# A fixed TensorE order for the experts' products, and one DVE place a unit for the weights' block sums

## Chip, cores and metric

One core of one Trainium2 chip. The metric is the device time of one execution in microseconds (us). The kernel before took 996.0 us in the median of three runs (993.51 to 996.29), and 994.75 us in the median of four.

## The reference, cut to what matters

```python
def _attn_ref(q, k, v):                     # linear attention, 8 batches x 8 heads x 576 x 64
    ...
def _moe_ref(x, w_gate, w1, w2):            # x: attention's output, 4608 x 512; 8 experts, hidden width 1024
    ...
    P = np.exp(logits)                      # logits from x @ w_gate; then 8 rounds of row and column scaling
    ...
    for e in range(E):
        h = np.maximum(x @ w1[e], 0.0)
        ye = h @ w2[e]
        out += P[:, e:e + 1] * ye
    ...
```

Every token goes through every expert. Attention, the gate and expert 0 take the first 193 us of the kernel before; experts 1 to 7 take the rest, and the change touches only them.

## The kernel before

All work is recorded as tasks with an engine, a guessed duration, dependencies and a priority. A list scheduler then replays time and emits the instructions in the order in which its own clock starts them. This is how TensorE's order comes about:

```python
            best = None
            for e, lst in avail.items():
                te = None
                for t in lst:
                    r = slot(t)
                    if r is None:
                        continue
                    s = max(free[e], r)
                    if te is None or s < te:
                        te = s
                if te is None:
                    continue
                pick = None
                for t in lst:
                    r = slot(t)
                    if r is not None and r <= te + 1e-9 and (pick is None or (t["prio"], t["id"]) < (pick["prio"], pick["id"])):
                        pick = t
                if best is None or te < best[0]:
                    best = (te, e, pick)
            ...
            t["fn"](e)          # emits the instructions of the task
```

A unit is 512 tokens through one expert. Each layer is a block product in seven products instead of eight, which needs sums of blocks of the inputs, of the weights and of h. Layer 1 of a unit is done in two halves, a and b (gi = 0, 1). A product here is four matmuls of 256 columns. The results stand in PSUM, the memory that matmuls write. The chain through the PSUM banks gX, gR and gZ fixes who waits for whom: the seed copy reads what m1 left in gX, and m6 may add its own result into gX only after it (`start` is false for m6). An instruction of ScalarE or VectorE that reads a bank like this is called an evictor below. In the text, a1 to a7 are the products m1 to m7 of half a, b1 to b7 those of half b, and y1 to y7 those of layer 2; the Python variables `a1`, `a5` and `a2` below are something else, the copies by ScalarE.

```python
            def pm(lhs, rhs, g_, first, deps, pr):
                def f_m(_):
                    if first:
                        pl, tag = kx[id(g_)]
                        g_["tile"] = pl.tile([P, 2, 256], FP32, tag=tag, name=tag)
                    dst = Zt[1] if g_ is gZ else g_["tile"]
                    for p in range(2):
                        for c in range(2):
                            nc.tensor.matmul(dst[:, p, :], lhsT=lhs(p, c), rhs=rhs(c),
                                             start=(first and p == 0 and c == 0), stop=(c == 1), skip_group_check=True)
                return add(("pe", 0.436), f_m, deps=deps, acq=[g_] if first else [], use=[g_, gw1, gW, gxs],
                           prio=ui + 0.35 + 0.35 * gi + pr)

            ...
            m1 = pm(A(1, 1, gi), B11, gX, True, tw1 + [tha, txs, prev_hq[0]], 0.0)
            prev_hq[0] = m1
            a1 = acts(f_seed, [m1], [gX], [gZ])
            m5 = pm(W(1, gi), T(1), gR, True, [m1, tW], 0.05)
            a5 = acts(f_s5, [m5, x_closed[0]], [gR], [gs5])
            m2 = pm(A(1, 2, gi), B21, gZ, False, [a1], 0.15)
            th[0].append(acts(f_h11, [m2], [gZ, gh]))
            m6 = pm(W(2, gi), T(2), gX, False, [a1, tW], 0.08)
            a2 = acts(f_s2, [m6, x_closed[0]], [gX], [gs2])
            m3 = pm(W(4, gi), B22, gR, False, [a5], 0.12)
            th[1].append(add(("dve", 0.69), f_h12, deps=[m3, a2], use=[gR, gs2, gh], prio=ui - 400.0))
            m7 = pm(W(3, gi), T(3), gX, False, [a2], 0.14)
            d22 = add(("dve", 0.69), f_h22, deps=[m7, a5], use=[gX, gs5, gh], prio=ui - 402)
            th[1].append(d22)
            m4 = pm(A(2, 2, gi), T(4), gX, False, [d22], 0.16)
            th[0].append(acts(f_h21, [m4], [gX, gh]))
```

Layer 2 (the y products, eight matmuls each) has the same form. Its products m5, m6, m3 and m7 read the blocks of S, which are sums of blocks of h:

```python
        m1 = pm(A(1, 1), Bq(1, 1), gX, True, th[0] + th[1], 0.0)
        c1 = add(("act", 0.58), f_seed, deps=[m1], acq=[gZ], use=[gX], prio=ui - 400.0)
        m5 = pm(SS(1), T(1), gR, True, [tS[0]], 0.1)
        e5 = ev(gR, 1, 1, m5)
        m2 = pm(A(1, 2), Bq(2, 1), gZ, False, [c1], 0.05)
        ev(gZ, 0, 0, m2, split=True)
        m6 = pm(SS(2), T(2), gX, False, [tS[1], c1], 0.2)
        e6 = ev(gX, 0, 1, m6)
        m3 = pm(SS(4), Bq(2, 2), gR, False, [tS[3]] + e5, 0.3)
        ev(gR, 0, 1, m3)
        m7 = pm(SS(3), T(3), gX, False, [tS[2]] + e6, 0.4)
        e7 = ev(gX, 1, 1, m7)
        m4 = pm(A(2, 2), T(4), gX, False, e7, 0.6)
        ev(gX, 1, 0, m4)
```

The sums of the weights' blocks, eight DVE instructions an expert, must be there before the expert's first unit. A lower number goes first, a unit's own number is its priority, and NG is the number of units of an expert (9): the sums ranked some four units ahead of the expert's own first unit:

```python
    def combos(e):
        gw1, tw1, gw2, tw2 = w_t[e]
        gT, gW = S_.grp(p_T), S_.grp(p_W)
        tW = tT = None
        for i in range(4):
            def f_W(_, i=i):
                if i == 0:
                    gW["tile"] = accp[1].tile([P, 4, 2, 512], FP16, tag="W", name="W")
                w, W = gw1["tile"], gW["tile"]
                a0, a1, op = [(w[:, 0:2, 512:1024], w[:, 2:4, 512:1024], ALU.add),
                              (W[:, 0], w[:, 0:2, 0:512], ALU.subtract),
                              (w[:, 0:2, 0:512], w[:, 0:2, 512:1024], ALU.subtract),
                              (w[:, 2:4, 0:512], W[:, 1], ALU.subtract)][i]
                nc.vector.tensor_tensor(out=W[:, i], in0=a0, in1=a1, op=op)
            tW = add(("dve", 0.685), f_W, deps=tw1 + [t_close, tW], acq=[gW] if i == 0 else [], use=[gw1, gW],
                     prio=NG * e - 4.5)
        for i in range(4):
            def f_T(_, i=i):
                if i == 0:
                    gT["tile"] = accp[2].tile([P, 4, 4, 256], FP16, tag="T", name="T")
                w, T = gw2["tile"], gT["tile"]
                a0, a1, op = [(w[:, 0:4, 256:512], w[:, 0:4, 0:256], ALU.subtract),
                              (w[:, 4:8, 256:512], T[:, 0], ALU.subtract),
                              (w[:, 4:8, 256:512], w[:, 0:4, 256:512], ALU.subtract),
                              (w[:, 4:8, 0:256], T[:, 1], ALU.subtract)][i]
                nc.vector.tensor_tensor(out=T[:, i], in0=a0, in1=a1, op=op)
            tT = add(("dve", 0.685), f_T, deps=tw2 + [x_closed[0], tT], acq=[gT] if i == 0 else [], use=[gw2, gT],
                     prio=NG * e - 4.0)
        return gW, tW, gT, tT

```

The softmax here doesn't subtract the row's maximum and nothing guards it: scores larger than these inputs give would overflow.

## Time and profile before

The times by stage come from the profile: the timeline's starts of the copy at L635, which seeds each half of each unit, tell where unit 9 (the first of expert 1) and unit 71 (the last of expert 7) begin.

| stage of the kernel before | us |
|---|---|
| to the first seed copy of unit 9 | 193.20 |
| from there to the first seed copy of unit 71 (62 units) | 772.92 |
| rest | 25.3 |
| span | 991.4 |

772.92 / 62 is 12.47 us a unit. The prediction shows the lines. In a line of the timeline the columns are start, duration, engine, source line, operation and operands; what stands in brackets is the idle time of the engine just ahead and what ended it. PE is TensorE (rows of matmuls, with modelled ends), PEld are its weight loads, DVE is VectorE, ACT is ScalarE, POOL is GpSimd and SPq a DMA issue.

### The profile page before, as it was taken

The page shows a single profiled execution, that of the slowest core. Times are in us where ns is not written, and L with a number is a line of the kernel's source. Part 1 is how long each engine was busy: PE and PEld are TensorE (multiplying, and loading weights), DVE is VectorE, ACT ScalarE, POOL GpSimd, SP SyncE. Part 2 cuts the span into 40 slices and gives each one's busy share as a digit, 9 for nine tenths or more (in the row PEclk, how much of TensorE's full clock was granted, in tenths as well). Part 3 has the DMA queues.
Part 4 walks back from the last instruction along what each step waited for, and adds up shares of the span by engine and source line. Part 5 has one row for each costly group of instructions (what it writes and reads, how often), then busy time and mean ns, then how long its engine had stood idle before and what let it go on. Part 6 is the DMA issues. An engine that isn't in the chain of part 4 may idle for free.

```text
span 991.4 us, 21411 instructions
## 1 busy us (share of the span) xinstructions
PE 965.9 (97%) x8716; PEld 789.4 (80%) x8716; DVE 771.6 (78%) x1561; ACT 562.5 (57%) x1034; POOL 131.6 (13%) x171
## 2 busy tenths in 40 slices
PE   7999999999999999999999999999999999999997
PEld 3556554488888888888888888888888888888885
DVE  6898879887777977797777977797777977777774
ACT  4898755555555555555555555555555555555552
POOL 5111100010111111111111111111111111111110
PEclk9999999999999999999999999999999999999999
DMA  9996952262226322271226322271225422236663
GB/s 308 290 299 220 286 177 107 67 136 76 75 67 128 101 78 79 78 164 55 66 72 137 97 75 76 77 160 72 75 76 122 114 75 76 75 101 162 162 162 98
DMA packets 47028, 121.99 MB, mean 123 GB/s; under 512 B 4176, under 2 KB 18000, under 8 KB 46928
## 3 DMA queue, kind: packets, MB, share of 16 engines
q1 hardware_dynamic: 32128, 99.76, 30.8%
q0 software_dynamic: 14480, 20.33, 11.5%
q8 instruction: 68, 1.11, 0.4%
q10 hardware_dynamic: 320, 0.52, 0.1%
q14 instruction: 32, 0.26, 0.1%
HBM read 119.69 MB, written 17.69 MB: 139 GB/s over the span
## 4 chain that ended last, share of the span: by engine, by line
PE 88%; DVE 6%; ACT 3%; DMA 1%; issue 1%; SPq 0%; ACTq 0%; DVEq 0%
PE ye L802 32%; PE hq L623 22%; PE att L623 10%; PE ye L699 6%; PE Zye L623 5%; PE Zye L802 5%; PE hq L532 4%; ACT Zye L635 1%; DVE tk L277 1%; DMA kin<-in_k_dram 1%; DVE tq L277 1%; DVE S L775 1%; DVE xn L372 1%; PE xt_ps L383 1%; DVE h L652 1%
## 5 line engine op out<-in xcount | busy, mean ns | idle before, releaser
L816 DVE SCALAR_TENSOR_TENSOR acc<-ye,P_sb,acc 128x256 f32<-128x256 f32 x620 | 266.6, 476 | 90.7 <-PE ye L802 76.4
L623 PEld LDWEIGHTS <-W 128*128 128x128 f16 x2016 | 196.7, 98 | 34.6 <-issue 11.2
L802 PEld LDWEIGHTS <-S 128*128 128x128 f16 x1984 | 192.1, 98 | 27.4 <-DVE S L775 3.8
L802 PE MATMUL ye<-T,S 128*128 128x256 f16 x1488 | 192.6, 273 | 0.0
L826 POOL TENSOR_TENSOR acc<-acc,st 128x256 f32<-128x256 f32 x124 | 91.1, 754 | 638.7 <-ACT st L823 628.7
L623 PEld LDWEIGHTS <-w 128*128 128x128 f16 x1512 | 147.5, 98 | 21.1 <-issue 1.0
L802 PEld LDWEIGHTS <-h 128*128 128x128 f16 x1488 | 145.4, 98 | 17.0
L623 PE MATMUL hq<-xs,W 128*128 128x256 f16 x1008 | 151.2, 273 | 6.5 <-ACT Zye L635 6.3
L623 PE MATMUL att<-xs,W 128*128 128x256 f16 x1008 | 151.2, 273 | 0.0
L623 PE MATMUL hq<-xs,w 128*128 128x256 f16 x1008 | 144.8, 273 | 0.8 <-DVE h L652 0.8
L649 ACT ACTIVATE h<-hq 128x512 f16<-128x512 f32 x126 | 76.3, 606 | 78.6 <-PE hq L623 78.6
L652 DVE CUSTOM_DVE_ANT_0 h<-att,s 128x512 f16<-128x512 f32 x126 | 86.5, 686 | 41.2 <-PE att L623 34.9
L775 DVE TENSOR_TENSOR S<-h 128x1024 f16<-128x1024 f16 x124 | 85.0, 685 | 41.1 <-ACT h L649 40.8
L646 ACT ACTIVATE h<-Zye 128x512 f16<-128x512 f32 x126 | 75.8, 602 | 54.4 <-PE Zye L623 54.2
L635 ACT COPY Zye<-hq 128x512 f32<-128x512 f32 x126 | 72.7, 577 | 58.7 <-PE hq L623 58.4
L643 ACT COPY s<-att 128x512 f32<-128x512 f32 x126 | 74.4, 590 | 46.1 <-PE att L623 45.9
L823 ACT ACTIVATE st<-Zye,P_sb 128x256 f32<-128x256 f32 x124 | 52.0, 470 | 75.2 <-PE Zye L802 75.2
L639 ACT COPY s<-hq 128x512 f32<-128x512 f32 x126 | 74.8, 593 | 24.3 <-PE hq L623 24.2
L652 DVE CUSTOM_DVE_ANT_0 h<-hq,s 128x512 f16<-128x512 f32 x126 | 86.2, 684 | 1.4 <-PE hq L623 1.0
L699 PE MATMUL ye<-w,h 128*128 128x512 f16 x320 | 76.9, 379 | 0.0
L623 PE MATMUL Zye<-xs,w 128*128 128x256 f16 x504 | 75.7, 273 | 0.0
L532 PE MATMUL hq<-xT,w 128*128 128x512 f16 x288 | 70.6, 379 | 2.4 <-ACT h L536 2.2
(90 smaller groups left out, 961.7 us busy)
## 6 DMA issues: line engine op xcount, KB each, us to landing
xs<-xd SPq DMA_DIRECT2D x63, 896.0 KB, 4.6
w<-in_moe_w_dram POOLq DMA_DIRECT2D x14, 1024.0 KB, 10.9
out_dram<-acc SPq DMA_DIRECT2D x68, 128.0 KB, 2.4
kin<-in_k_dram SPq DMA_DIRECT2D x14, 576.0 KB, 6.0
qin<-in_q_dram SPq DMA_DIRECT2D x14, 576.0 KB, 5.3
vin<-in_v_dram SPq DMA_DIRECT2D x14, 576.0 KB, 6.3
xd<-xst SPq DMA_DIRECT2D x9, 512.0 KB, 2.6
xd<-xT SPq DMA_DIRECT2D x9, 256.0 KB, 6.8
```

The source lines that it names most:

```text
L532: nc.tensor.matmul(ghq["tile"], lhsT=gw1["tile"][:, c, ts(f, P)], rhs=xT[:, c, ds(512 * g, 512)], start=(c == 0), stop=(c == NDT - 1))
L623: nc.tensor.matmul(dst[:, p, :], lhsT=lhs(p, c), rhs=rhs(c), start=(first and p == 0 and c == 0), stop=(c == 1), skip_group_check=True)
L635: nc.scalar.copy(out=Zt[1], in_=gX["tile"])
L639: nc.scalar.copy(out=gs2["tile"], in_=gX["tile"])
L646: nc.scalar.activation(out=hd(0, 0), in_=Zt[1], func=AF.Relu)
L649: nc.scalar.activation(out=hd(1, 0), in_=gX["tile"], func=AF.Relu)
L652: nc.vector._custom_dve(TENSOR_ADD_SAT, out=dst, in0=ps, in1=sb, s0=3.0e38, s1=0.0)
L699: nc.tensor.matmul(gy[tt]["tile"], lhsT=gh["tile"][:, f, ds(P * tt, P)], rhs=gw2["tile"][:, f, :], start=(f == 0), stop=(f == NFT - 1))
L775: nc.vector.tensor_tensor(out=Sx[:, i], in0=a0, in1=a1, op=op)
L802: nc.tensor.matmul(bank(g_)[:, s, :], lhsT=lhs(s, kk), rhs=rhs(kk), start=(new and s == 0 and kk == 0), stop=(kk == 3), skip_group_check=True)
L816: nc.vector.scalar_tensor_tensor(out=dst(), in0=bank(g_)[:, s, :], scalar=P_sb[:, gg, e:e + 1], in1=dst(), op0=ALU.mult, op1=ALU.add)
L826: nc.gpsimd.tensor_tensor(out=dst(), in0=dst(), in1=gst["tile"], op=ALU.add)
```

## The change

Its intent is to pin the faster of the two repeating orders that the scheduler had found for TensorE, and to take the block sums out of bursts. A chain of dependencies orders all products of experts 1 to 7 by one pattern (y of the unit before, a and b of the unit, A for a of the next one), 28 slots of four matmuls a unit. Each block sum of the next expert waits for the b half's second add (b22) of one unit of the expert before and then goes first on DVE. The diff, cut:

```diff
@@ class _Plan
+    def dep(self, k, d):
+        self.t[d]["kids"].append(k)
+        self.t[k]["nd"] += 1
@@ block7, pair(): pm
-                           prio=ui + 0.35 + 0.35 * gi + pr)
+                           prio=ui + (0.35 if ui > NG else -2.0) + 0.35 * gi + pr)
@@ block7, pair(): end
+            for n, t in zip("1234567", (m1, m2, m3, m4, m5, m6, m7)):
+                pe_id[(ui, f"{'ab'[gi]}{n}")] = t
+            pe_id[(ui, f"{'ab'[gi]}22")] = d22
@@ combos: W, then T likewise
-            tW = add(("dve", 0.685), f_W, deps=tw1 + [t_close, tW], acq=[gW] if i == 0 else [], use=[gw1, gW],
-                     prio=NG * e - 4.5)
+            tW = add(("dve", 0.685), f_W, deps=tw1 + [t_close, tW, pe_id.get((NG * (e - 1) + i + 1, "b22"))], acq=[gW] if i == 0 else [], use=[gw1, gW],
+                     prio=-900.0 if e > 1 else 4.5)
-            tT = add(("dve", 0.685), f_T, deps=tw2 + [x_closed[0], tT], acq=[gT] if i == 0 else [], use=[gw2, gT],
-                     prio=NG * e - 4.0)
+            tT = add(("dve", 0.685), f_T, deps=tw2 + [x_closed[0], tT, pe_id.get((NG * (e - 1) + i + 5, "b22"))], acq=[gT] if i == 0 else [], use=[gw2, gT],
+                     prio=-900.0 if e > 1 else 5.0)
@@ unit: the y products are entered in pe_id in the same way (cut)
@@ end
+    order = "y1 y5 y2 y6 a7 y3 y7 a4 b1 b5 y4 b6 b3 b2 b7 A1 A5 b4 A6 A3 A2".split()
+    chain = []
+    for u in range(NG - 1, E * NG + 1):
+        for n in order:
+            key = (u - 1, n) if n[0] == "y" else (u + 1, n.lower()) if n[0] == "A" else (u, n)
+            if key in pe_id:
+                chain.append(pe_id[key])
+    for d, k_ in zip(chain, chain[1:]):
+        S_.dep(k_, d)
     S_.run()
```

More of the change, by code (lines that the diff above doesn't have):

```diff
@@ L850, in unit @@
         m4 = pm(A(2, 2), T(4), gX, False, e7, 0.6)
+        for n, t in zip("1234567", (m1, m2, m3, m4, m5, m6, m7)):
+            pe_id[(ui, f"y{n}")] = t
         ev(gX, 1, 0, m4)
@@ L857 @@
     xd_done, xs_prev, x_closed = {}, [None], [None]
+    pe_id = {}
     for g in range(NG):
```

## The prediction

> **What bounds the kernel now.** A "unit" is 512 tokens through one expert: layer 1 in two halves a and b of seven products each (four matmuls of 256 columns a product), layer 2 (y) in seven products of eight matmuls. That is 112 matmuls, or 28 slots of four. Experts 1 to 7 have 63 units, numbered 9 to 71; products carry their numbers in the diff (a1, b4, y5). I read the page first: busy shares and the chain that ended last.
>
> ```profile
> span 991.4 us, 21411 instructions
> ...
> PE 965.9 (97%) x8716; PEld 789.4 (80%) x8716; DVE 771.6 (78%) x1561; ACT 562.5 (57%) x1034; POOL 131.6 (13%) x171
> ...
> PE 88%; DVE 6%; ACT 3%; DMA 1%; issue 1%; SPq 0%; ACTq 0%; DVEq 0%
> ```
>
> TensorE is the bound, and only 3% seems left. A matmul's recorded end is modelled, so short stops hide inside "busy". I therefore took the timeline and listed every start of the copy that seeds a half (L635, one for each half of each unit). Units come in two rhythms: 12.74 us for units 10, 12 to 18, 30 to 36 and 48 to 54 (22), and 12.30 us for 21 to 27, 39 to 45 and 57 to 70 (28), with mixed units between. The view of stretches shows seven units of each kind:
>
> ```profile
> 454.10:543.26 89.16, 87.23 (x787) 75.98 (x785) 64.81 (x127) 47.86 (x91) 11.59 (x16) 1.00 0.30 87
> 806.27:892.35 86.08, 86.08 (x787) 76.56 (x785) 64.23 (x127) 47.89 (x92) 9.88 (x14) 1.00 0.26 83
> ```
>
> Columns: length, then busy time and count of PE, PEld, DVE, ACT, POOL, then clock, DMA. The same 787 recorded matmuls at the same clock 1.00 take 3.08 us less in the second. The weight loads, whose spans are not padded, say where. The waits of PEld in the first stretch (the second has none):
>
> ```profile
> PEld L623 <- issue: 3.2, 7, 0.5
> PEld L802 <- DVE S L775: 1.3, 7, 0.2
> ```
>
> One slow unit in the timeline:
>
> ```profile
> 504.79 0.60 PE L623 MATMUL att<-xs,W 128*128 128x256 f16 x4
> 505.05 0.57 ACT L635 COPY Zye<-hq 128x512 f32<-128x512 f32 x1 [1.54 <-PE hq L623]
> 505.67 0.60 PE L623 MATMUL hq<-xs,W 128*128 128x256 f16 x4 [0.28 <-ACT Zye L635]
> 505.67 0.32 PEld L623 LDWEIGHTS <-W 128*128 128x128 f16 x3 [0.45 <-issue]
> ...
> 509.22 0.77 PEld L802 LDWEIGHTS <-S 128*128 128x128 f16 x8 [0.18 <-DVE S L775]
> ```
>
> a6 overwrites the bank that the seed copy reads. The order is a1 (504.35), a5 (504.79), a6: it could start at 505.23 (504.79 + 0.437) and starts at 505.67, so 0.44 us is lost. At 509.22 y5 waits for the first S block, some 0.06 us. One fast unit, where b4 stands between a5 and a6:
>
> ```profile
> 592.71 0.69 DVE L652 CUSTOM_DVE_ANT_0 h<-hq,s 128x512 f16<-128x512 f32 x1
> 592.95 0.60 PE L623 MATMUL att<-xs,W 128*128 128x256 f16 x4
> 593.46 0.60 PE L623 MATMUL hq<-xs,w 128*128 128x256 f16 x4
> ...
> 594.16 0.62 ACT L649 ACTIVATE h<-hq 128x512 f16<-128x512 f32 x1
> ...
> 594.81 0.69 DVE L775 TENSOR_TENSOR S<-h 128x1024 f16<-128x1024 f16 x1 [1.41 <-ACT h L649]
> ...
> 596.07 1.04 PE L802 MATMUL ye<-T,S 128*128 128x256 f16 x8
> ```
>
> b4 (593.46) could have started at 592.95 + 0.437 = 593.39: 0.07 us of stall, behind the DVE add that ends at 593.40. Nothing else stalls. Note DVE's idle 1.41 us before the S block, and that y5 (596.07) starts 0.57 us after that block ends (594.81 + 0.69).
>
> **What the Trainium skill says.** (1) "TensorE: Matmul & The Clock Gate", "Step-by-step: what each phase is for": only weight loads are pulled ahead; matmuls stay in program order. The trace agrees: at 505.67 all of TensorE stands behind one copy. So the written order decides how much other work lies between a product and the evictor it needs: two slots between a1 and a6 are 0.87 us, and the copy needs 1.32 (504.35 to 505.67); three are 1.31. (2) Same page, "Wait — 56ns, not 53.3ns?": warm spacing is N / 2.4 GHz + about 2.5 ns, which is 109.2 ns for 256 columns, 12.23 us for 112. The fast rhythm is 12.297 with 0.07 of stall seen, 12.23 without: it agrees, so the fast rhythm is at the floor of this instruction mix. (3) "Perfetto Trace Analysis", "Tensor Engine Instruction (MATMUL, LD_WEIGHTS)": the end of a matmul is an estimate; so it is here, four matmuls of 0.60 us following each other every 0.437. (4) "SBUF — State Buffer", "SBUF: two separate sides": a DVE instruction with two SBUF inputs and a GpSimd one that reads SBUF exclude each other. The trace fits: where block sums fall beside GpSimd's adds (324.17) two adds take 1.98 us instead of 1.41. At the new place GpSimd is idle (its adds at 598.65 to 600.06).
>
> **The change part by part.** It adds and removes no work: instruction counts of every engine are equal. I built the changed kernel and compared the orders.
>
> *TensorE.* From unit 10 to the end every unit has the sequence a1 a5 (old b4) a6 a3 a2 y1 y5 y2 y6 a7 y3 y7 a4 b1 b5 y4 b6 b3 b2 b7. This is exactly, product for product, what the scheduler had found in the 12.30 us units. ACT's and DVE's orders around it are those of the fast units too. So I need no new timetable: the rhythm has been measured in 28 units of this very kernel.
>
> *The block sums* (eight instructions of 0.685 us an expert). Before, all eight fell within some two and a half units, squeezed between S blocks and evictions; each such burst throws the pattern from one rhythm to the other (fast to slow at expert 4's and 6's, slow to fast at 3's, 5's, 7's). Now there is one a unit, in eight units, just behind b's second add and before S. In the fast unit that add ends at 593.40; a sum ends at 593.40 + 0.69 = 594.09, and S may start only at 594.81. It fits with 0.7 us over: cost 0. Critical loop of the fast rhythm (b6, copy 0.59, add 0.69, add 0.69, b4) lies before it.
>
> *Unit 9's start.* The orders are the same until 193.4 us. Then expert 0's six remaining half products are spread between unit 9's instead of bunched. Placing them by hand, I find every eviction done before its reader: for instance the copy for a7 ends at 195.6 and a7 comes at 196.4. Work from a1 of unit 9 (192.51) to a1 of unit 10: 13 slots x 0.437 + 6 x 0.863 (24 matmuls from 193.38 to 198.56) = 10.86; before it took 11.05 (203.56). Saved: 0.2.
>
> *The sum*, each stretch between equal places, against 12.297 a unit:
> units 10 to 20: 203.56 to 342.55 (a1) = 138.99 against 135.26: 3.7.
> units 28 to 38: 429.31 to 568.61 (seed) = 139.30: 4.0.
> units 46 to 56: 654.68 to 793.98 = 139.30: 4.0.
> The units between and 57 to 70 already run at 12.30: 0.
> With unit 9: 12.0 us. Four fifths of it (9.7) is 22 slow units x 0.44, the rest the mixed units around the bursts. The tail (unit 71's plain layer 2, with a 0.78 us wait for DVE) is ordered as before.
>
> **The rivals.**
> (A) The sums delay S, and so y5. Against: the slack is 1.41 - 0.69 idle, then 0.57 at y5. Were the sum on the path after all, 48 sums x 0.69 = 33 us: about 1017.
> (B) A sum waits for weights still in flight, and DVE, a FIFO, stands behind it. For: one weight load landed only 13.0 us after its issue. Against: w1's buffer comes free at the last b4 of the expert before last, about 1.3 us into an expert's first unit; the first sum comes after unit two's b half, over 24 us later; w2 has even more. If true, up to some us an expert: gain gone, about 990 to 996.
> (C) A fixed order gives a new stall elsewhere, as the xs load (4.6 us) or a bank. Against: the same order ran for 14 units in a row, across an expert's boundary at unit 63, without change. A rhythm of 12.5 would leave nothing (61 x 0.2 = 12).
> (D) A fuller TensorE lowers the clock. Against: 1.00 in the fast stretches.
>
> **Range and chances.** The span should fall from 991.4 to 979.4. The three timed runs were 993.5, 996.0 and 996.3 (the profiled one 993.2), so the level itself wanders by 2.8 us; 996.0 - 12.0 = 984.0, from the lower level 981.5. I say 983.5, with 979.5 to 987.5 for the wander and for a transient of 1 to 3 us at the start. Faster by 2% would need 20 us, more than all the stalls I can find (12.0, plus 62 x 0.07 = 4 that remain); slower needs (A). Chances: faster 0.01, same 0.98, slower 0.01.
>
> **What would show it.** Seed copies of the a halves 12.30 us apart throughout, the b half 8.80 after the a half; TensorE's wait for L635 (6.3 us in the page's waits) and the weight load's wait for S (3.8) gone; a block sum within DVE's former 1.41 us gap and S still released by ACT L649; TensorE's busy share up to 98%. I am wrong if the period is above 12.35, if S or y5 starts later after b4 than now (1.35 and 2.61), or if DVE waits for a weight load.

## The result, and the profile after

The changed kernel took 984.25 us (median of four runs, 983.97 to 984.51), the kernel before 994.75. The ratio is 0.9894 with a 95% interval of 0.9875 to 0.9913. In a later set of rounds the pair stood at 981.83 and 994.13 (0.9878).

The page of the changed kernel, busy shares and the chain that ended last:

```profile
span 982.2 us, 21403 instructions
...
PE 962.2 (98%) x8716; PEld 792.7 (81%) x8716; DVE 771.7 (79%) x1561; ACT 563.2 (57%) x1034; POOL 127.9 (13%) x171
...
PE 89%; DVE 1%; ACT 1%; issue 0%
```

Busy time of every engine is what it was, within 0.6% for all but POOL; only the span around it is shorter. DVE's share of the chain that ended last fell from 6% to 1%, ACT's from 3% to 1%. The stretches view gives units 30 to 36, which ran in the slow rhythm before, and units 57 to 63, which ran in the fast one (columns as in the prediction):

```profile
452.71:538.83 86.12, 86.12 (x787) 76.65 (x785) 68.43 (x134) 47.91 (x92) 11.61 (x16) 1.00 0.31 91
784.74:870.81 86.07, 86.07 (x787) 76.65 (x785) 68.44 (x134) 47.91 (x91) 9.88 (x14) 1.00 0.22 76
```

The first took 89.16 us before, the second 86.07. DVE has 134 recorded instructions instead of 127: one block sum in each of the seven units. The starts of the seed copies are 12.29 or 12.30 us apart from unit 11 on (unit 10: 12.32), with two exceptions, unit 21 (12.53) and unit 31 (12.35). The b half comes 8.80 to 8.82 us after the a half, but for units 9 (6.55) and 21 (9.04). One unit in the timeline, with a block sum (L761):

```profile
599.82 0.69 DVE L656 CUSTOM_DVE_ANT_0 h<-hq,s 128x512 f16<-128x512 f32 x1
...
600.05 0.60 PE L627 MATMUL att<-xs,W 128*128 128x256 f16 x4
...
600.42 0.68 DVE L761 TENSOR_TENSOR T<-w 128x1024 f16<-128x1024 f16 x1
600.56 0.60 PE L627 MATMUL hq<-xs,w 128*128 128x256 f16 x4
...
601.91 0.69 DVE L782 TENSOR_TENSOR S<-h 128x1024 f16<-128x1024 f16 x1 [0.81 <-ACT h L653]
...
603.18 1.04 PE L809 MATMUL ye<-T,S 128*128 128x256 f16 x8
```

The sum sits right behind b's second add, ends at 601.10, and DVE is still idle for 0.81 us before S. S starts 1.35 us after b4 (601.91 - 600.56) and y5 2.62 us after it; in the fast units before it was 1.35 and 2.61. From 190 to 970 us the view of TensorE's waits holds a single line for the matmuls, at the last b4 of unit 71; the 6.3 us for the seed copy are gone. So are the 3.8 us in which weight loads waited for S: what is left of their waits is 0.3 us in unit 21 and 1.0 at that last b4, both put down to "issue". DVE waits for no transfer there.

```profile
PE hq L627 <- DVE h L656: 0.8, 1, 0.8
```

| stage | before | after |
|---|---|---|
| to the first seed copy of unit 9 | 193.20 | 195.68 |
| 62 units | 772.92 | 761.20 |
| rest | 25.3 | 25.3 |
| span | 991.4 | 982.2 |

The 62 units gained 11.7 us. The first stage lost 2.5 us although its instructions and their order are the same in both programs. It varies from run to run: over the ten profiles, all with this same first stage, its end lies between 193.20 and 196.55. Five of them, the changed kernel's among them, show 3.4 us of granted clock 0.50 within the first 21 us (11.70 to 15.11 here); these five end at 193.66 to 196.55, the other five at 193.20 to 193.71. That is at most a part of the difference, as 3.4 us at half clock can cost 1.7; the rest was not followed up.

### The profile page after: what moved, and what is told of

The parts are those of the page before. It is cut to its first block, busy times and chain, and to the rows that moved or that the text cites. A ratio compares the mean times of both kernels' runs of the same rounds, so it can differ in the third digit from the quotient of the medians. Undisturbed runs are those within 1.5% of the kernel's fastest.

```text
span 982.2 us, 21403 instructions
## 1 busy us (share of the span) xinstructions
PE 962.2 (98%) x8716; PEld 792.7 (81%) x8716; DVE 771.7 (79%) x1561; ACT 563.2 (57%) x1034; POOL 127.9 (13%) x171
## 4 chain that ended last, share of the span: by engine, by line
PE 89%; DVE 1%; ACT 1%; issue 0%
PE ye L809 33%; PE hq L627 23%; PE att L627 11%; PE Zye L627 6%; PE Zye L809 6%; PE ye L706 5%; PE hq L536 4%; PE xt_ps L387 0%; PE kv_ps L306 0%; PE num_ps L371 0%; PE lg_ps L405 0%; DVE tk L281 0%; PE qt_ps L332 0%; ACT tq L272 0%; PE den_ps L347 0%; ACT qpT L221 0%
## 5 line engine op out<-in xcount | busy, mean ns | idle before, releaser
L809 PEld LDWEIGHTS <-S 128*128 128x128 f16 x1984 | 194.1, 98 | 22.7 <-issue 0.3
L833 POOL TENSOR_TENSOR acc<-acc,st 128x256 f32<-128x256 f32 x124 | 87.5, 725 | 625.6 <-ACT st L830 620.7
L627 PE MATMUL hq<-xs,w 128*128 128x256 f16 x1008 | 140.7, 272 | 0.8 <-DVE h L656 0.8
## 6 DMA issues: line engine op xcount, KB each, us to landing
w<-in_moe_w_dram POOLq DMA_DIRECT2D x14, 1024.0 KB, 11.7
```

Of the source, the lines that this page charges most:

```text
L627: nc.tensor.matmul(dst[:, p, :], lhsT=lhs(p, c), rhs=rhs(c), start=(first and p == 0 and c == 0), stop=(c == 1), skip_group_check=True)
L809: nc.tensor.matmul(bank(g_)[:, s, :], lhsT=lhs(s, kk), rhs=rhs(kk), start=(new and s == 0 and kk == 0), stop=(kk == 3), skip_group_check=True)
L833: nc.gpsimd.tensor_tensor(out=dst(), in0=dst(), in1=gst["tile"], op=ALU.add)
```

## The experiments

Every edit is against the changed kernel. For each run the length from the first seed copy of unit 9 to the second one of unit 71 is given ("the expert phase"), as it leaves out the noise of the start: 781.73 us before (193.20 to 974.93) and 770.01 after (195.68 to 965.69). sums_only, order_only, b4_late and new_order ran on one chip, the other four on another; each is compared with the kernel before of its own rounds.

### The sums alone

```diff
-                           prio=ui + (0.35 if ui > NG else -2.0) + 0.35 * gi + pr)
+                           prio=ui + 0.35 + 0.35 * gi + pr)
...
-    for d, k_ in zip(chain, chain[1:]):
-        S_.dep(k_, d)
```

> The order chain is left out; the block sums keep their one place a unit. Built, the scheduler by itself falls into the same repeating order from unit 11 on, with DVE and ACT as in the changed kernel. My theory (it is the rhythm that counts, and bursts of block sums are what throws the scheduler from one rhythm to the other): the seed copies of the a halves 12.30 us apart from unit 11 on, and from unit 9's first seed copy to unit 71's last one 770.0 to 770.8 us (changed kernel 770.0, before 781.7); time 984 to 985, ratio to before 0.989 to 0.991. Rival (the pinned order is what brings the gain): no better than 990.

Measured: 983.19 us (981.84 to 985.03), ratio to before 0.9887 (0.9871 to 0.9902), expert phase 770.3 us, period 12.22 in unit 10 and 12.30 from unit 11 on, with the same two exceptions in units 21 (12.54) and 31. Period and phase are as expected, the time is 0.8 us under the expected range. The waits of the weight loads from 190 to 960 us:

```profile
PEld L627 <- issue: 0.4, 2, 0.2
PEld L809 <- issue: 0.3, 1, 0.3
```

Neither is a wait for an evictor in the repeating pattern. So the chain of dependencies adds nothing measurable to the gain: with the sums spread, the scheduler finds the same order by itself and keeps it across all six borders between experts. The chain and the raised priority of unit 9's products, which this run drops together, are worth 0.3 us of the phase, in units 9 and 10. One sum a unit at some other place was not tried, so the runs don't tell how much of this is the spreading and how much the place behind b22.

### The order alone

```diff
-            tW = add(("dve", 0.685), f_W, deps=tw1 + [t_close, tW, pe_id.get((NG * (e - 1) + i + 1, "b22"))], ...
-                     prio=-900.0 if e > 1 else 4.5)
+            tW = add(("dve", 0.685), f_W, deps=tw1 + [t_close, tW], ...
+                     prio=NG * e - 4.5)
   (T in the same way, prio=NG * e - 4.0)
```

> The order is pinned, the block sums stay in bursts of eight over some two units, as before the change. My theory: TensorE keeps the 12.30 us order between the bursts, so most of the gain stays; a burst of 8 x 0.685 = 5.5 us meets some 3.1 us of DVE idle time a unit (12.3 - 9.2) in two units, so each of the six bursts costs little, 0.3 to 1.5 us: first to last seed copy 772 to 779 us, time 986 to 993. Rival (placing the sums is what matters): as before, 781 us, 994.75.

Measured: 999.58 us (999.04 to 1003.39), ratio to before 1.0056 (1.0039 to 1.0073), expert phase 787.87 us. This is 6 us worse than before, and both theories missed it. Between the bursts the period is 12.30, as I had said. But units 28, 37, 46 and 55 take 14.63 us, unit 11 takes 16.55 and unit 19 takes 16.30. My working had asked only whether DVE has room for the sums, not which instruction stands behind them. DVE and TensorE in unit 28, from the timeline:

```profile
438.08 0.68 DVE L749 TENSOR_TENSOR W<-w 128x1024 f16<-128x1024 f16 x1
...
440.06 0.68 DVE L749 TENSOR_TENSOR W<-w,W 128x1024 f16<-128x1024 f16 x1
440.15 0.60 PE L627 MATMUL hq<-xs,W 128*128 128x256 f16 x4
...
442.18 0.68 DVE L782 TENSOR_TENSOR S<-h,S 128x1024 f16<-128x1024 f16 x1
442.91 1.64 PEld L809 LDWEIGHTS <-S 128*128 128x128 f16 x16 [2.44 <-DVE S L782]
442.92 1.05 PE L809 MATMUL ye<-w,S 128*128 128x256 f16 x8 [2.17 <-DVE S L782]
```

a7 starts at 440.15 and y3 could start at 440.59. It needs the fourth S block. That block stands on DVE behind two sums, an add and two evictions, and ends at 442.86, so y3 starts at 442.92: 2.33 us lost. In the kernel before, the scheduler met such a burst by bringing other products forward; that is how the mixed units with their 12.56 or 13.55 us came about (in the order that it built for unit 28, b1, b5, a4 and b6 stand ahead of y7 and y3). A pinned order cannot do that.

Units 11 and 19 lost another 1.7 us each. The stretches view shows the time just after the stop in units 11, 19 and 28 (the clock is the column behind the last busy time):

```profile
220.20:224.20 4.00, 3.98 (x22) 2.92 (x22) 2.38 (x4) 1.50 (x3) 0.00 (x0) 0.57 0.49 138
329.50:333.00 3.50, 3.50 (x20) 2.51 (x18) 2.88 (x7) 1.13 (x2) 0.00 (x0) 0.52 0.00 0
442.90:447.00 4.10, 4.08 (x38) 3.67 (x39) 4.03 (x8) 1.60 (x3) 0.00 (x0) 1.00 0.00 0
```

In two of the cases the granted clock fell: 0.57 over 4.00 us is 3.4 us at half speed (4.00 x 0.43 / 0.5), and so is 0.52 over 3.50. Half of 3.4 is the 1.7 us. The last section takes this up. The idle times in the profile were 2.2 to 2.5 us long, and four of six had no such consequence. Unit 11's stop has one more cause: DVE stood 2.3 us behind a sum that waited for its weights, which is rival (B) of the prediction, come true here and not in the changed kernel, whose list of DVE's waits in the expert phase holds no wait for a transfer. The overruns, 0.5 + 4.25 + 4.0 + 4 x 2.33 = 18.1 us, agree with the 17.9 us by which the phase is longer than that of the changed kernel.

### b4 one place later

```diff
-    order = "y1 y5 y2 y6 a7 y3 y7 a4 b1 b5 y4 b6 b3 b2 b7 A1 A5 b4 A6 A3 A2".split()
+    order = "y1 y5 y2 y6 a7 y3 y7 a4 b1 b5 y4 b6 b3 b2 b7 A1 A5 A6 b4 A3 A2".split()
```

> The pinned order with b4 moved one place back, behind a6 of the next unit: a1 a5 a6 b4 in place of a1 a5 b4 a6; all else as in the changed kernel. My theory (distance between a1 and a6): a6 again waits 0.44 us for the seed copy in every unit, b4's 0.07 us wait goes, and S, which comes later behind a later b4, makes y5 wait some 0.3 us: period 12.9 to 13.05 in place of 12.30, so 61 x 0.6 to 0.75 = 37 to 46 us more: time 1021 to 1031, slower than before. Rival (a fixed order is good as such): within 3 us of 984.

Measured: 1028.38 us (1026.31 to 1029.19), ratio to before 1.0337, expert phase 814.48 us, period 13.01 in every unit (13.26 in unit 21). The waits of the weight loads from 190 to 960 us, which hold 58 units:

```profile
PEld L809 <- DVE S L782: 26.3, 58, 0.5
PEld L627 <- issue: 26.3, 58, 0.5
```

One wait for a6 and one for y5 in each unit, as expected: 13.01 - 12.30 = 0.71, which is 0.44 at a6 and some 0.34 at y5, less the 0.07 that b4 no longer waits. The order is just as fixed as in the changed kernel and contains the same work. One exchange of two products costs 44 us of the expert phase. So it is the distance between a1 and a6, and between b4 and y5, that makes the rhythm. The wait at a6 looks as in the slow units before:

```profile
504.02 0.57 ACT L639 COPY Zye<-hq 128x512 f32<-128x512 f32 x1 [0.27 <-PE hq L627]
...
504.64 0.60 PE L627 MATMUL hq<-xs,W 128*128 128x256 f16 x4 [0.28 <-ACT Zye L639]
```

### The sums twice, and four times

```diff
-                nc.vector.tensor_tensor(out=W[:, i], in0=a0, in1=a1, op=op)
+                for _r in range(2 if e > 1 else 1):      # 4 in the second kernel
+                    nc.vector.tensor_tensor(out=W[:, i], in0=a0, in1=a1, op=op)
   (T in the same way)
```

> Each block sum of experts 2 to 7 is computed twice (the same values written again) in its place between b's second add and S. My theory (the gap of 1.41 us holds it): two sums end 0.60 + 0.69 = 1.29 us after the add, before S is released at 1.41; period 12.30 in all units, time within 1.5 us of the changed kernel. Rival (the sums lie on the path): 48 x 0.6 = 29 us more, 1013.

Measured: 981.29 us (981.08 to 981.83), against 981.83 for the unaltered changed kernel of the same rounds; expert phase 769.75 us. The 48 added sums cost nothing. One pair in the timeline, and the S block behind it:

```profile
597.98 1.41 DVE L763 TENSOR_TENSOR T<-w 128x1024 f16<-128x1024 f16 x2
599.47 0.69 DVE L784 TENSOR_TENSOR S<-h 128x1024 f16<-128x1024 f16 x1
```

> Each block sum four times. Theory: four sums end 3 x 0.60 + 0.69 = 2.49 us after the add; S starts there in place of 1.41 us, 1.08 later, of which 0.57 is slack before y5: y5 waits 0.5 us in the 48 units that hold a sum (period 12.8) and not in the others: 48 x 0.5 = 24 us more, time 1003 to 1016. TensorE's wait for S in y5 appears in 48 places and no other. Rival (DVE, at 9.2 + 2.4 of 12.3 us a unit, has room): 984.

Measured: 1024.99 us (1024.74 to 1025.47), ratio to before 1.0306, expert phase 813.14 us. The place was right and the size was not: the 48 units with a sum take 13.20 us and the others 12.30, so 0.90 us each in place of 0.5. One such unit:

```profile
597.04 2.86 DVE L750 TENSOR_TENSOR W<-w 128x1024 f16<-128x1024 f16 x4
597.18 0.60 PE L627 MATMUL hq<-xs,w 128*128 128x256 f16 x4
...
599.82 0.69 DVE L784 TENSOR_TENSOR S<-h 128x1024 f16<-128x1024 f16 x1
...
600.56 1.05 PE L811 MATMUL ye<-T,S 128*128 128x256 f16 x8 [0.60 <-DVE S L784]
```

I had taken 0.60 us from one sum to the next, which is the spacing of S blocks in the timeline (596.02 to 596.62 in the kernel before); four sums into the same place take 2.86, so 0.72 each. S ends at 600.51 (599.82 + 0.69), and y5 starts 3.38 us after b4 (600.56 - 597.18) in place of 2.61: 0.77 lost. The other 0.13 is at y3, which waits for the fourth S block. The waits confirm it: the weight loads wait for S 96 times, twice in each of 48 units. Together the two runs measure the room of the chosen place: one more sum is free, three more are not; two more were not tried.

### Another order, against the last stall

The changed kernel still loses 0.07 us a unit at b4.

```diff
-    order = "y1 y5 y2 y6 a7 y3 y7 a4 b1 b5 y4 b6 b3 b2 b7 A1 A5 b4 A6 A3 A2".split()
+    order = "y1 y5 y2 y6 a7 y3 b1 b5 a4 y7 b6 b2 b3 b7 y4 A1 A5 b4 A6 A3 A2".split()
```

> Another fixed order, which should also remove the last stall (b4 waits 0.07 us a unit for the chain b6, copy, add, add): b1 and b5 three places earlier, y7 between a4 and b6, y4 between b7 and the next a1, b7 behind b3: y1 y5 y2 y6 a7 y3 b1 b5 a4 y7 b6 b2 b3 b7 y4 a1 a5 b4 a6 a3 a2. b6 to b4 is then eight slots (3.5 us) instead of six (2.62), against a chain of 2.7 to 2.9. Theory: period 12.23 to 12.25, 61 x 0.05 to 0.07 = 3 to 4 us less than the changed kernel: first to last seed copy 766 to 767, time 980 to 981.5. If 12.297 is a floor for another reason, or a new wait appears: 984 or more.

Measured: 981.63 us (981.24 to 982.36), ratio to before 0.9871, period 12.29 or 12.30 as in the changed kernel: a miss. The expert phase of 768.27 us is shorter by 1.7 us, but mostly because the last unit's b half comes sooner after its a half (7.43 us in place of 8.80); 0.3 more is that units 21 and 31 show no irregularity in this run. The stall had moved by two products:

```profile
611.02 0.60 PE L627 MATMUL att<-xs,W 128*128 128x256 f16 x4
611.27 0.57 ACT L639 COPY Zye<-hq 128x512 f32<-128x512 f32 x1 [1.58 <-PE hq L627]
611.46 0.60 PE L627 MATMUL hq<-xs,w 128*128 128x256 f16 x4
611.76 0.59 ACT L647 COPY s<-att 128x512 f32<-128x512 f32 x1
611.90 0.60 PE L627 MATMUL hq<-xs,W 128*128 128x256 f16 x4
612.40 0.60 PE L627 MATMUL att<-xs,W 128*128 128x256 f16 x4
```

b4 (611.46) and a6 (611.90) follow at 0.44 us without a gap, a3 (612.40) at 0.50. It needs the second copy, which ends at 612.35. In the changed kernel b4's stall had covered this one. So three chains there are within some 0.07 us of each other, and taking away one shows the next.

### The order with more distance

```diff
-            m1 = pm(A(1, 1, gi), B11, gX, True, tw1 + [tha, txs, prev_hq[0]], 0.0)
+            m1 = pm(A(1, 1, gi), B11, gX, True, tw1 + [txs, prev_hq[0]], 0.0)
   (tha goes to the three kinds of task that write h: f_h11, f_h12, f_h22)
-    order = "y1 y5 y2 y6 a7 y3 y7 a4 b1 b5 y4 b6 b3 b2 b7 A1 A5 b4 A6 A3 A2".split()
+    order = "y1 y5 y2 y6 a7 y3 b1 b5 a4 y7 b6 b2 b3 b7 A1 A5 y4 b4 A6 A3 A2".split()
```

> In the last new order the 0.07 us wait of b4 was gone and a3 waited 0.06 us in its place, for the second copy behind the seed (a1 to a3 four slots = 1.75 us, needed 1.81). Here y4 stands between a5 and b4, so that a1 to a6 is five slots and a1 to a3 six (2.6 us), b7 to b4 five; the first product of a unit no longer waits in the scheduler for the tile of h, which it does not write. Theory (waits alone keep the period above 112 x 109.2 ns): period 12.23, 61 x 0.065 = 4 us less: first seed copy of unit 9 to that of unit 71 757 us in place of 761; time 3 to 4.5 us below the changed kernel of the same rounds, 980 to 981. Rival (the stalls only move on, or 12.297 is the floor): within 1.5 us of it.

> The changed kernel unaltered, as the measure for the three beside it on the same chip: 984 (982 to 985.5), ratio to before 0.989; period 12.30.

Measured in the same rounds: 977.26 us (976.82 to 977.56) with the new order, 981.83 (981.77 to 984.36) for the changed kernel unaltered; ratios to before 0.9825 (0.9808 to 0.9842) and 0.9878 (0.9858 to 0.9897). The new one over the changed kernel is 0.9825 / 0.9878 = 0.9946. Both medians lie just outside what was expected: the changed kernel 0.2 us under its 982 to 985.5, the gain with 4.57 us just over its 3 to 4.5. The period is 12.22 or 12.23 from unit 11 on; unit 10 takes 11.44, as its y4 now stands behind the next a1. The stretches view over nearly the whole expert phase shows no idle time of TensorE's matmuls at all:

```profile
189.50:960.00 770.50, 770.50 (x7021) 686.78 (x7020) 605.53 (x1177) 431.25 (x821) 97.84 (x136) 1.00 0.36 100
```

The views of TensorE's waits are empty there. With modelled ends this alone would prove little (the changed kernel's fast stretch shows no idle time either, and b4 stalls in it). The proof is the period: 12.226 / 112 = 109.2 ns a matmul, which is the warm spacing that the prediction worked with. This version, correct and faster than both, is at the floor of its instruction mix, and what is left lies outside the units' rhythm. Its two edits, the order and the dependency on tha, were not run apart.

## Why the prediction was right, point by point

*The bound and the two rhythms.* Confirmed. The slow rhythm is gone in every unit, and b4_late brought its a6 stall back by one exchange in the order. One reading was off: the prediction told slow units by their length alone, and units 10 and 12 are not slow ones. In the kernel before, the stall of 0.44 us at a6 stands in 23 places, in units 13 to 19, 30 to 37 and 48 to 55, 10.1 us in all. Units 10 and 12 lose only 0.20 us there, and the order that the scheduler built gives each of them 29 slots in place of 28 (29 x 0.437 = 12.67), which makes them about as long as the slow ones. So "22 slow units x 0.44" is not the right split of the 12.0 us; the sum itself is not touched, as it is worked out from whole stretches.

*Units 10 to 56, 11.8 us, and unit 9, 0.2 us.* The 62 units gave 11.7 us in place of 12.0. From a1 of unit 9 to a1 of unit 10 the trace shows 10.85 us (194.99 to 205.84) against 10.86 worked out. The missing 0.3 us are two single irregularities, 0.23 us in unit 21, which for this one unit is above the prediction's own limit of 12.35, and 0.05 in unit 31. They recur in the same units of other runs (12.54 and 12.35 in the second run of the changed kernel), though not in all; in unit 21 a weight load waits for "issue", that is for nothing that the profile shows, and the 0.05 us of unit 31 show up in no wait. Their cause is left open.

*The sums cost 0 in their place.* Confirmed, and its room measured: twice the sums is free, four times costs 43 us. What the prediction says of GpSimd's adds at 324.17 needs a correction: no block sum falls beside them. The instruction there is an S block (L775, 324.34), which the burst of sums had pushed back, and it takes 1.22 us in place of 0.68. It too has two inputs in SBUF, so it fits the page that the prediction names just as well.

*The time.* 984.25 us against 983.5 predicted, within 979.5 to 987.5. That it came within 0.75 us is in part luck: the same kernel took 981.83 in the later rounds. The gap between the medians was 10.5 us in the first comparison and 12.3 in the later one; the start stage, which ends up to 3.4 us sooner or later from profile to profile, is enough to explain that they differ from the phase's 11.7, but single timed runs have no stages to show it.

*The rivals.* (A), (B) and (D) did not occur in the expert phase of the changed kernel, where the granted clock is 1.00; of (C) there is nothing beyond the 0.3 us of units 21 and 31. (A) is what four sums do, and (B) is among what the order alone does. The clock of (D) fell there too, but behind stops of TensorE and not because it was fuller.

*What the prediction did not separate.* It named bursts as what throws the scheduler from one rhythm to the other, but it put the pinned order first, and its sum does not say which part brings the 12 us. The experiments do: spreading the sums is sufficient alone (expert phase 770.3 us), and the pinned order alone loses 6.1 us (787.87 against 781.73). My expectation for the order alone was wrong in its term for a burst, 0.3 to 1.5 us, which measured 2.33 to 4.25. That spread sums keep the good rhythm from unit 11 on was also read from the built order, before that run; the chip only confirmed its duration.

## What to carry to other kernels

When an engine looks 97% busy, compare equal pieces of work by the starts of one recurring instruction: two rhythms of the same loop give the possible gain and the order that earns it without any model. Check that the pieces hold the same work, though: units 10 and 12 were as long as slow ones and held one product more. For each pair of products that are tied through an evictor, count the slots between them against the evictor's time (here 1.32 us of copy needs just over three slots of 0.437), and expect several chains to be nearly equal, so that removing one stall only shows the next. Place occasional work by what stands behind it in its engine's queue, not by that engine's average idle time; and do not pin one engine's order while irregular work on another still moves what it waits for.

## What the Trainium skill lacked or had wrong

- "TensorE: Matmul & The Clock Gate", section "Back-to-back issue gap": it says of N / 2.4 GHz + 2.5 ns that it holds for an isolated gap only and counts too much at large N in a stream of weight loads and matmuls (131 ns at N = 512). Here, in such a stream, it holds: 109.2 ns at N = 256 over some 60 units of 112 matmuls without a stall (new_order2), and 215.8 ns at N = 512 (24 matmuls from 193.38 to 198.56 in the kernel before). Nothing near 131 ns was seen.
- The same page, section "HAM oscillation — how this bites in real kernels": its rule of no idle gap above some 3.4 us is too generous. Stops of TensorE of some 2.3 to 2.7 us (from the last matmul's start plus 0.109 to the next start) were followed by 3.4 us at half clock in two cases of six, which cost another 1.7 us each. The traces suggest which two. The stretches at half clock run from 220.23 to 223.65 and from 329.46 to 332.87 and start 109.23 us apart, 32 times their length of 3.41. If the clock is decided in steps of this length, laid end to end, then the step just before held 2.67 and 2.20 us of stop in these two cases, while the stops of the other four were cut by the edge between two steps, with at most 1.96 us in one. This fits all six, but it is inferred from six cases and was not tested.
- No page gives the spacing of two DVE sums of this form of which the second waits for the first. It would belong to "VectorE: DVE Perf Modes", whose passage on waits between instructions measures copies. It is 0.72 us for a sum of 128x1024 f16 repeated into its own output, against 0.60 for S blocks into different ones. In the trace each repeated sum waits for a semaphore of the sum before it and starts some 35 ns after its end, while an S block starts before the one ahead has ended. A sum into another place that reads the one just written is as late (0.73, 216.17 to 216.90 in order_only), so it seems to be the wait and not the place; that was not tested.
